# Attention followed by two feed-forward blocks: the halves of a head's values summed by a DMA in SBUF, and x loaded as one operand

## The chip, the cores and the metric

One core of one Trainium2 chip. The metric is device time in microseconds of one execution, lower is better. The engines are named as the profile does: PE is TensorE's matmul, PEld its weight load, DVE is VectorE, ACT is ScalarE, POOL is GpSimd, SP is SyncE, which here only issues DMAs; SPq is its queue.

## What is computed

Attention over 4 batches of 8 heads, 576 positions of 64 values, with scores further than tau below a row's maximum dropped; then a gated feed-forward block (512 to 1536 to 512) and a bilinear one, on 2304 tokens, all in float32.

```python
scores = (q @ k.T) / sqrt(64)                       # per batch and head
thresh = scores.max(-1, keepdims=True) - tau
scores = where(scores >= thresh, scores, -1e9)
attn = exp(scores - scores.max(-1, keepdims=True))
attn = attn / (attn.sum(-1, keepdims=True) + 1e-9)
x = (attn @ v).transpose(0, 2, 1, 3).reshape(2304, 512)
g = x @ w_gate; x = (g * sigmoid(g) * (x @ w_val)) @ moe_w_out
out = (((x @ w1) * (x @ w2)) @ w3) @ moe2_w_out
```

## The kernel before

Each float32 operand is split into a high and a low part in a format that TensorE multiplies at full rate, and a product is three matmul passes (high by high, high by low, low by high). The split costs ScalarE a copy (the high part) and VectorE or POOL a subtraction (the low part).

*Attention* runs in 16 passes, one for each batch and pair of heads (`p`, batch `p // 4`, pair `p % 4`), of 9 tiles of 128 queries each. For a tile: scores (L440), row maximum while they are copied out (VectorE, L479), exponential (ScalarE, L488), threshold for two tiles at a time (POOL, L471), mask and row sum (VectorE, L498; it stands two tiles behind the scores). The masked probabilities are turned by TensorE (L326) and split as they leave PSUM (L510 to L536), and multiplied with the values (L579, L584). The values stand as two parts side by side in the weights, so the result of a head has 128 rows: 64 from the high part of the values, 64 from the low part. ScalarE copies it into `xs` (L591, two buffers), and SP stores the two halves into `x_dram[0]` and `x_dram[1]` in DRAM (L595), two DMAs per head, four per pass. The reciprocal row sums of a batch go into `r_dram` (`it_norm`, L610 and L613).

Meanwhile the operands of the next pass are prepared: q and k are loaded (L281), turned, split, and stacked by twelve SBUF-to-SBUF DMAs (L349, L350: R<-khi, R<-klo, L<-qhi, L<-qlo) on SP. Rows of the profile with `L` and `R` are these tiles; `P` holds the scores, `AT` the turned probabilities.

*The first feed-forward block* reads x as blocks of 512, 512, 256, 512 and 512 tokens, each in four parts of 128 features: 20 preparations, `x_prep(j, kk)`. One takes two operand slots; SP loads both halves of x into the one (L785) and the reciprocal sums, spread over 64 rows, into the other (L790); POOL adds the halves (L821), VectorE multiplies by the reciprocals (L824), ScalarE writes the high part (L812), VectorE the low part (L813). The first four preparations are queued in the last pass of attention, the others in the entry into the block, between the steps `glu_step`: the projections (L830), the gate (L914, L915, and the split L107, L108), and the output products, accumulated in PSUM and added to SBUF by VectorE (L877) or, at first, copied by ScalarE (L879). Weights are loaded raw and split beside it (L140 to L200; `raw`, `tmp`).

*What sets the order.* The kernel issues the work of a pass through two queues of items with credits (`some`): `main` for the turning and the products, `prep` for the next pass's operands. A framework then simulates the program and fixes an order for each engine; on the chip each engine runs its own list in that order, and an instruction that waits holds up all that stand behind it. A DMA is issued by the engine whose list it stands in, when that engine comes to it. At the start `LZ` and `VLZ` are filled with zeros (L249, L253), and tau is loaded and its sign and positive part are taken (L656, L659).

Of the kernel before, what the change touches and what calls it, by code (L numbers as in the profile page):

```python
# [9 lines left out]
F32 = mybir.dt.float32  # L10
# [4 lines left out]
ALU = mybir.AluOpType  # L15
# [21 lines left out]
def kernel(  # L37
# [42 lines left out]

    x_dram = dram.tile([2, DM, B, S], F32, name="x_dram")
    r_dram = dram.tile([B, H, S], F32, name="r_dram")
# [151 lines left out]
    def attention(actx, early, tail):  # L234
# [13 lines left out]
        LZ = at.tile([P, 2, 3 * P], F32R, name="LZ")  # L248
        nc.gpsimd.memset(f32(LZ), 0.0)  # L249

        VLZ = [at.tile([P, HP, 2, 2, D], F32R, name=f"VLZ{n}") for n in range(2)]
        for t in VLZ:
            nc.gpsimd.memset(f32(t), 0.0)  # L253

# [314 lines left out]
        def it_pv(p, h, n):  # L569
# [22 lines left out]
            if n == 1:  # L592
                g = 2 * hp + h
                for e in range(2):
                    nc.sync.dma_start(  # L595
                        out=x_dram[e, g * D:(g + 1) * D, b, :], in_=xs[64 * e:64 * e + 64, :]
                    )

# [54 lines left out]
        load_left(0)  # L653
        nc.sync.dma_start(out=tau_sb, in_=tau.to_broadcast([P, 1]))

# [49 lines left out]
        for n, (p, i) in enumerate(tiles):  # L705
            b, hp = divmod(p, HP)
            if i == 0:
# [6 lines left out]
                if p + 1 < NP:  # L714
                    prep.extend(prep_items(p + 1))
                    credit[1] = 0.0
            if i == NTILE - 2:
# [62 lines left out]
    def x_load(j, kk):  # L780
        c0, n = blocks[j]
        x_raw[j, kk] = [take(F32) for _ in range(2)]
        tt, rg = x_raw[j, kk]
        for o, b, c, m in segs(c0, n):
            nc.sync.dma_start(  # L785
                out=tt[:, :, o:o + m],
                in_=x_dram[:, kk * P:(kk + 1) * P, b, c:c + m].rearrange("e p c -> p e c"),
            )
            for h in range(2):
                nc.sync.dma_start(  # L790
                    out=rg[64 * h:64 * h + 64, 0, o:o + m],
                    in_=r_dram[b, 2 * kk + h:2 * kk + h + 1, c:c + m].to_broadcast([64, m]),
                )
        return tt, rg

# [21 lines left out]
    def x_prep(j, kk):  # L817
        c0, n = blocks[j]
        tt, rg = x_load(j, kk)
        xr = tmp()  # L820
        nc.gpsimd.tensor_tensor(  # L821
            out=xr[:, 0:n], in0=tt[:, 0, 0:n], in1=tt[:, 1, 0:n], op=ALU.add
        )
        nc.vector.tensor_tensor(out=xr[:, 0:n], in0=xr[:, 0:n], in1=rg[:, 0, 0:n], op=ALU.mult)  # L824
        give(*x_raw.pop((j, kk)))
        x_split(j, kk, xr[:, 0:n])
# [299 lines left out]
```

## Time and profile before

| what | value |
|---|---|
| time, median of 3 runs | 1182.14 us (1175.77 to 1183.02) |
| the profiled execution's own time | 1180.05 us |
| its span in the trace | 1177.6 us |
| mean granted clock of TensorE | 0.993 |
| PE, PEld busy | 1112.7 us (94%), 952.4 us (81%) |
| DVE, ACT, POOL busy | 747.4 us (63%), 577.8 us (49%), 443.2 us (38%) |

The profiled execution is one run of the same program. Its span begins with its first instruction and ends with its last; the other 2.45 us of its time lie around the span. All rows below are of this execution. Attention ends at about 349 us; the entry into the first feed-forward block reaches to about 440 us.

### The profile page before, as it was taken

Reading aid. Unit: us, or ns where it says so; the run is one execution under the profiler, and the core shown is the slowest. Engines: PE = TensorE matmul, PEld = TensorE weight load, DVE = VectorE, ACT = ScalarE, POOL = GpSimd, SP = SyncE. Lnnn points to the kernel's source line nnn. Section 1 sums busy time; section 2 is a strip of 40 time slices with the busy share of each in tenths; the row PEclk is TensorE's granted clock in tenths of the full one; section 3 lists DMA queues with packets and bytes.
Section 4 is the critical chain, followed back from the end, with each engine's and each line's share of the span. In section 5 each row is a group of like instructions: output and inputs, shape, how many; then the busy total and the mean of one; then the engine's idle time right before and its main releaser. Section 6 shows DMA issues by size and latency. Waiting matters only on the chain.

```text
span 1177.6 us, 16738 instructions
## 1 busy us (share of the span) xinstructions
PE 1112.7 (94%) x6044; PEld 952.4 (81%) x6044; DVE 747.4 (63%) x1317; ACT 577.8 (49%) x1041; POOL 443.2 (38%) x434
## 2 busy tenths in 40 slices
PE   6898879989988899999999999999999999999998
PEld 5787779888876688888888888888787888888886
DVE  7999898999986786665463655477891122522222
ACT  5787777878876355434232432344662231321111
POOL 5456355645444555343241432234342221321110
PEclk9999999999999999999999999999999999999999
DMA  9865675755555832221120120133330010100023
GB/s 212 191 137 131 148 165 120 179 131 133 136 160 141 247 105 90 90 72 54 36 58 32 54 72 19 42 99 99 119 109 18 1 36 1 36 1 1 1 60 101
DMA packets 105330, 107.07 MB, mean 91 GB/s; under 512 B 48288, under 2 KB 79648, under 8 KB 105248
## 3 DMA queue, kind: packets, MB, share of 16 engines
q1 hardware_dynamic: 105248, 106.01, 34.4%
q8 instruction: 47, 0.77, 0.3%
q14 instruction: 35, 0.29, 0.1%
HBM read 68.16 MB, written 14.23 MB: 70 GB/s over the span
## 4 chain that ended last, share of the span: by engine, by line
PE 64%; DVE 17%; DMA 8%; issue 3%; POOL 2%; SPq 2%; ACT 2%; DVEq 0%; POOLq 0%; ACTq 0%
PE t_bank L830 36%; PE s_bank L830 19%; DVE P L498 4%; PE t_bank L579 4%; DVE P L479 3%; PE s_bank L440 2%; DMA raw<-in_moe_w_dram 2%; DMA L<-qlo 2%; PE t_bank L326 2%; DVE slot L813 1%; DMA slot<-r_dram 1%; DVE tmp L158 1%; PE t_bank L584 1%; DMA slot<-x_dram 1%; DVE tmp L824 1%
## 5 line engine op out<-in xcount | busy, mean ns | idle before, releaser
L830 PE MATMUL t_bank<-slot,slot 128*128 128x512 f32 (+1 forms) x2592 | 561.1, 372 | 5.7 <-DVE slot L813 2.0
L830 PEld LDWEIGHTS t_bank<-slot,slot 128*128 128x128 f32 x2592 | 458.3, 189 | 92.2 <-DVE slot L813 3.0
L830 PE MATMUL s_bank<-h,slot 128*128 128x512 f32 (+1 forms) x720 | 161.2, 371 | 7.2 <-DVE slot L877 3.6
L151 POOL TENSOR_TENSOR raw<-raw 128x512 int32<-128x512 int32 x76 | 85.1, 1120 | 191.2 <-ACT raw L150 181.6
L830 PEld LDWEIGHTS s_bank<-h,slot 128*128 128x128 f32 x720 | 126.8, 190 | 31.4 <-ACT tmp L914 3.7
L498 DVE SCALAR_TENSOR_TENSOR P<-P,stat,E 128x576 f32<-128x576 f32 x144 | 144.5, 1017 | 12.0 <-POOL stat L471 7.2
L1062 DVE TENSOR_TENSOR tmp<-tmp,t_bank 128x512 f32<-128x512 f32 (+1 forms) x40 | 25.4, 634 | 178.2 <-PE t_bank L830 178.2
L488 ACT ACTIVATE E<-P,stat 128x576 f32<-128x576 f32 x144 | 113.7, 792 | 28.9 <-DVE P L479 26.5
L108 POOL TENSOR_TENSOR h<-tmp,h 128x512 fp32r<-128x512 f32 (+1 forms) x60 | 74.9, 1248 | 127.0 <-ACT h L107 127.0
L1066 POOL TENSOR_TENSOR h<-tmp,h 128x512 fp32r<-128x512 f32 (+1 forms) x38 | 45.8, 1205 | 200.8 <-ACT h L1064 200.8
L479 DVE TENSOR_SCALAR_CACHE_REDUCE P<-s_bank,neg 128x576 f32<-128x576 f32 x144 | 114.9, 807 | 8.1 <-PE s_bank L440 7.4
L440 PE MATMUL s_bank<-R,L 128*128 128x288 f32 x512 | 99.3, 315 | 21.9 <-DVE P L479 10.1
L830 PE MATMUL s_bank<-slot,h 128*128 128x512 f32 x432 | 106.6, 391 | 0.9 <-DVE slot L1052 0.8
L915 DVE TENSOR_TENSOR tmp<-tmp,t_bank 128x512 f32<-128x512 f32 (+1 forms) x60 | 37.9, 632 | 107.1 <-PE t_bank L830 100.4
L440 PEld LDWEIGHTS s_bank<-R,L 128*128 128x128 f32 x512 | 74.3, 190 | 33.1 <-DVE P L479 18.2
L326 PE MATMUL t_bank<-ident,P 128*128 128x128 f32 x640 | 92.3, 278 | 9.2 <-DVE klo L343 2.9
L830 PEld LDWEIGHTS s_bank<-slot,h 128*128 128x128 f32 x432 | 79.9, 188 | 18.3 <-DVE slot L1052 2.1
L877 DVE TENSOR_TENSOR slot<-s_bank,slot 128x1024 f32<-128x1024 f32 (+1 forms) x72 | 82.5, 1147 | 18.5 <-PE s_bank L830 16.5
L158 DVE SCALAR_TENSOR_TENSOR tmp<-tmp,raw 128x512 f32<-128x512 f32 x76 | 68.9, 906 | 40.0 <-POOL raw L151 40.0
L326 PEld LDWEIGHTS t_bank<-ident,P 128*128 128x128 f32 x640 | 73.3, 141 | 18.7 <-DVE klo L343 4.4
L149 ACT ACTIVATE raw<-raw,ebias 128x512 int32<-128x512 int32 x76 | 58.0, 765 | 59.9 <-DVE tmp L146 47.4
L914 ACT ACTIVATE tmp<-t_bank 128x512 f32<-128x512 f32 (+1 forms) x60 | 33.3, 555 | 109.9 <-PE t_bank L830 104.2
(103 smaller groups left out, 1393.6 us busy)
## 6 DMA issues: line engine op xcount, KB each, us to landing
raw<-in_moe_w_dram SPq DMA_DIRECT2D x32, 512.0 KB, 3.8
raw<-in_moe_w_out_dram SPq DMA_DIRECT2D x20, 512.0 KB, 3.5
x_dram<-xs SPq DMA_DIRECT2D x64, 144.0 KB, 2.4
L<-qlo SPq DMA_DIRECT2D x60, 128.0 KB, 2.6
L<-qhi SPq DMA_DIRECT2D x60, 128.0 KB, 2.6
raw<-in_moe_w_gate_dram SPq DMA_DIRECT2D x12, 512.0 KB, 3.9
raw<-in_moe_w_val_dram SPq DMA_DIRECT2D x12, 512.0 KB, 3.8
ld<-in_k_dram SPq DMA_DIRECT2D x16, 256.0 KB, 3.6
```

Of the source, the lines that this page charges most:

```text
L108: nc.gpsimd.tensor_tensor(out=lo, in0=src, in1=f32(hi), op=ALU.subtract)
L149: nc.scalar.activation(out=a, in_=x, func=ACTF.Relu, scale=8.0, bias=ebias[:, 0:1])
L151: nc.gpsimd.tensor_tensor(out=a, in0=a, in1=x, op=ALU.subtract)
L158: nc.vector.scalar_tensor_tensor(out=f32(m), in0=f32(m), scalar=2.0 ** 20, in1=f32(a), op0=ALU.add, op1=ALU.mult)
L326: nc.tensor.matmul(bank[:, t * P:(t + 1) * P], lhsT=part, rhs=ident, is_transpose=True, start=(t == 0), stop=(t == len(parts) - 1),)
L440: nc.tensor.matmul(o, lhsT=lhs, rhs=R[:, c:c + HALF], start=(h == hs2[0] and e == 0), stop=(h == hs2[-1] and e == 1),)
L479: nc.vector.tensor_scalar(out=p_tile(p, i).rearrange("p (a c) -> p a c", a=2), in0=sb[:, :, 0:HALF], scalar1=neg, scalar2=None, op0=ALU.mu ...
L488: nc.scalar.activation(out=e, in_=p_tile(p, i), func=ACTF.Exp, scale=-1.0, bias=stats[p // HP][:, 0, c:c + 1],)
L498: nc.vector.scalar_tensor_tensor(out=t, in0=t, scalar=stats[b][:, 1, c:c + 1], in1=e, op0=ALU.is_le, op1=ALU.mult, accum_out=sums[b][:, c: ...
L579: nc.tensor.matmul(o, lhsT=vs[:, 4 * h + c, :, :].rearrange("p a d -> p (a d)"), rhs=AT[h][:, e, c, cs], start=(c == 0 and e == 0), stop=F ...
L830: nc.tensor.matmul(o, lhsT=lhs(a), rhs=rhs(c), start=(first and i == 0), stop=(last and i == 2))
L877: nc.vector.tensor_tensor(out=a, in0=s, in1=a, op=ALU.add)
```

## The change

- `x_dram` has one half. Once both parts of a head's `xs` are copied, POOL issues a DMA that adds rows 64 to 127 of `xs` onto rows 0 to 63 within SBUF, and SP stores rows 0 to 63. Per pass two DMAs on POOL and two on SP stand for four on SP.
- `x_load` takes one slot: x in its first half, the reciprocals in its second. The POOL add is gone; VectorE multiplies the two halves of the slot.
- The zero fills of `LZ` and `VLZ` go from POOL to VectorE.
- The load of tau goes from SP's queue to ScalarE's.
- The credit of the preparation queue starts at -1.5 instead of 0 in pass 0, so the operands of pass 1 are prepared later in it.

```diff
-    x_dram = dram.tile([2, DM, B, S], F32, name="x_dram")
+    x_dram = dram.tile([DM, B, S], F32, name="x_dram")
...
-        nc.gpsimd.memset(f32(LZ), 0.0)
+        nc.vector.memset(f32(LZ), 0.0)
...
-            nc.gpsimd.memset(f32(t), 0.0)
+            nc.vector.memset(f32(t), 0.0)
...
                 g = 2 * hp + h
-                for e in range(2):
-                    nc.sync.dma_start(
-                        out=x_dram[e, g * D:(g + 1) * D, b, :], in_=xs[64 * e:64 * e + 64, :]
-                    )
+                nc.gpsimd.dma_start(out=xs[0:64, :], in_=xs[64:P, :], accum_op=ALU.add)
+                nc.sync.dma_start(out=x_dram[g * D:(g + 1) * D, b, :], in_=xs[0:64, :])
...
-        nc.sync.dma_start(out=tau_sb, in_=tau.to_broadcast([P, 1]))
+        nc.scalar.dma_start(out=tau_sb, in_=tau.to_broadcast([P, 1]))
...
-                    credit[1] = 0.0
+                    credit[1] = 0.0 if p else -1.5
...
-        x_raw[j, kk] = [take(F32) for _ in range(2)]
-        tt, rg = x_raw[j, kk]
+        t = x_raw[j, kk] = take(F32)
         for o, b, c, m in segs(c0, n):
             nc.sync.dma_start(
-                out=tt[:, :, o:o + m],
-                in_=x_dram[:, kk * P:(kk + 1) * P, b, c:c + m].rearrange("e p c -> p e c"),
+                out=t[:, 0, o:o + m], in_=x_dram[kk * P:(kk + 1) * P, b, c:c + m]
             )
             for h in range(2):
                 nc.sync.dma_start(
-                    out=rg[64 * h:64 * h + 64, 0, o:o + m],
+                    out=t[64 * h:64 * h + 64, 1, o:o + m],
...
-        tt, rg = x_load(j, kk)
+        t = x_load(j, kk)
         xr = tmp()
-        nc.gpsimd.tensor_tensor(
-            out=xr[:, 0:n], in0=tt[:, 0, 0:n], in1=tt[:, 1, 0:n], op=ALU.add
-        )
-        nc.vector.tensor_tensor(out=xr[:, 0:n], in0=xr[:, 0:n], in1=rg[:, 0, 0:n], op=ALU.mult)
-        give(*x_raw.pop((j, kk)))
+        nc.vector.tensor_tensor(
+            out=xr[:, 0:n], in0=t[:, 0, 0:n], in1=t[:, 1, 0:n], op=ALU.mult
+        )
+        give(x_raw.pop((j, kk)))
```

How the change moves the lists of the engines, at three places. A row is the line, the operation, output <- inputs and the shape; in the changed kernel the lines behind the edits are 2 to 5 lower (L824 is L817, L813 is L809, L915 is L910, L877 is L872; L594 is the accumulating DMA).

POOL where pass 6 ends and pass 7 begins; `sp` are the values' high and low parts of the next pass. Before:

```order
L104 TENSOR_TENSOR AT<-tmp,AT 128x512
L471 TENSOR_SCALAR stat<-stat,tau_sb 128x2
L101 TENSOR_SCALAR sp_2673<-ld_2093 128x8x64
L104 TENSOR_TENSOR sp_2673<-ld_2093,sp_2673 128x8x64
L471 TENSOR_SCALAR stat<-stat,tau_sb 128x2
```

The changed kernel, at the same place:

```order
L471 TENSOR_SCALAR stat<-stat,tau_sb 128x2
L594 DMA xs<-xs 64x576
L101 TENSOR_SCALAR sp_2673<-ld_2093 128x8x64
L104 TENSOR_TENSOR sp_2673<-ld_2093,sp_2673 128x8x64
L594 DMA xs<-xs 64x576
L471 TENSOR_SCALAR stat<-stat,tau_sb 128x2 x2
```

The two accumulating DMAs stand among the thresholds; each waits for ScalarE's copy of its `xs`, and two thresholds follow the second.

SP where pass 7 ends, the end of the second batch. Before:

```order
L595 DMA x_dram<-xs 64x576 x4
L610 DMA r_dram<-rt 8x4x128
L613 DMA r_dram<-rt 8x1x64
L274 DMA ld_2971<-in_v_dram 128x2x256
L281 DMA ld_3033<-in_k_dram 128x8x64
L281 DMA ld_3035<-in_q_dram 128x8x64
L349 DMA R<-khi 64x512
L350 DMA R<-khi 64x512
```

The changed kernel, at the same place:

```order
L595 DMA x_dram<-xs 64x576
L608 DMA r_dram<-rt 8x4x128
L611 DMA r_dram<-rt 8x1x64
L274 DMA ld_2971<-in_v_dram 128x2x256
L281 DMA ld_3033<-in_k_dram 128x8x64
L595 DMA x_dram<-xs 64x576
L349 DMA R<-khi 64x512
L350 DMA R<-khi 64x512
```

The four stores became two, and the second, which waits for its accumulate, stands right ahead of the twelve stacking DMAs.

VectorE in the entry into the first feed-forward block, at the preparations of the third and fourth block of tokens. Before:

```order
L824 TENSOR_TENSOR tmp<-tmp,slot_5098 128x256
L813 TENSOR_TENSOR slot_5080<-tmp,slot_5080 128x256
L824 TENSOR_TENSOR tmp<-tmp,slot_5111 128x256
L915 TENSOR_TENSOR tmp<-tmp,t_bank 128x512
L813 TENSOR_TENSOR slot_5081<-tmp,slot_5081 128x256 x2
L824 TENSOR_TENSOR tmp<-tmp,slot_5174 128x512
L915 TENSOR_TENSOR tmp<-tmp,t_bank 128x512
L824 TENSOR_TENSOR tmp<-tmp,slot_5191 128x512
L813 TENSOR_TENSOR slot_5184<-tmp,slot_5184 128x512
```

The changed kernel, at the same place:

```order
L817 TENSOR_TENSOR tmp<-slot_5077 128x256
L817 TENSOR_TENSOR tmp<-slot_5088 128x256
L809 TENSOR_TENSOR slot_5062<-tmp,slot_5062 128x256 x2
L809 TENSOR_TENSOR slot_5063<-tmp,slot_5063 128x256 x2
L910 TENSOR_TENSOR tmp<-tmp,t_bank 128x512
L817 TENSOR_TENSOR tmp<-slot_5149 128x512
L809 TENSOR_TENSOR slot_5158<-tmp,slot_5158 128x512
L817 TENSOR_TENSOR tmp<-slot_5164 128x512
L910 TENSOR_TENSOR tmp<-tmp,t_bank 128x512
```

The multiplies read a landed slot instead of POOL's sum, and stand a little further ahead of the subtractions.

## Rows read from the trace of the kernel before

**Rows 1.** The page, busy time, share of the span and instructions of each engine.

```profile
PE 1112.7 (94%) x6044; PEld 952.4 (81%) x6044; DVE 747.4 (63%) x1317; ACT 577.8 (49%) x1041; POOL 443.2 (38%) x434
```

**Rows 2.** Windows: length, busy PE PEld DVE ACT POOL (instructions), clock, DMA share, GB/s.

```profile
15.00:330.00 315.00, 280.10 (x2010) 253.50 (x2011) 292.43 (x661) 250.76 (x499) 161.55 (x193) 0.99 0.65 151
...
350.00:380.00 30.00, 25.44 (x134) 20.62 (x135) 19.78 (x29) 19.83 (x35) 10.68 (x8) 0.98 0.54 145
380.00:396.00 16.00, 14.93 (x62) 11.93 (x61) 10.48 (x14) 6.58 (x11) 9.34 (x9) 0.92 0.78 221
396.00:413.00 17.00, 12.71 (x68) 10.99 (x69) 14.36 (x20) 5.98 (x13) 10.98 (x9) 0.91 0.90 256
...
440.00:800.00 360.00, 359.89 (x1764) 304.71 (x1764) 206.76 (x278) 138.99 (x223) 127.47 (x107) 1.00 0.19 59
```

**Rows 3.** Lines by form, 350 to 440 us: busy us, mean ns, idle before.

```profile
L821 POOL TENSOR_TENSOR tmp<-slot 128x512 f32<-128x512 f32 x12 | 17.5, 1464 | 15.0 <-DMA slot<-r_dram 10.8 <-DMA slot<-x_dram 3.0 <-DVE slot L813 1.2
...
L824 DVE TENSOR_TENSOR tmp<-tmp,slot 128x512 f32<-128x512 f32 x13 | 15.1, 1172 | 4.7 <-POOL tmp L821 3.3 <-DMA slot<-r_dram 1.3
L813 DVE TENSOR_TENSOR slot<-tmp,slot 128x512 fp32r<-128x512 f32 x13 | 14.5, 1120 | 0.9 <-ACT slot L812 0.7
```

**Rows 4.** Timeline of DVE: start, length, instruction, idle before and its releaser.

```profile
402.54 0.68 DVE L824 TENSOR_TENSOR tmp<-tmp,slot 128x512 f32<-128x512 f32 x1
403.14 3.46 DVE L813 TENSOR_TENSOR slot<-tmp,slot 128x512 fp32r<-128x512 f32 x2
...
414.38 1.78 DVE L824 TENSOR_TENSOR tmp<-tmp,slot 128x512 f32<-128x512 f32 x1
```

**Rows 5.** Lines by form, DVE, 440 to 640 us.

```profile
L200 DVE TENSOR_TENSOR slot<-tmp,slot 128x512 fp32r<-128x512 f32 x11 | 9.8, 888 | 6.0 <-ACT slot L197 6.0
```

**Rows 6.** Timeline of PE in the entry.

```profile
378.35 0.73 PE L830 MATMUL s_bank<-h,slot 128*128 128x512 f32 x2 [1.91 <-ACT h L107]
...
408.82 2.07 PE L830 MATMUL s_bank<-h,slot 128*128 128x512 f32 x6 [3.57 <-DVE slot L877]
```

**Rows 7.** Timeline of POOL at the end of attention.

```profile
345.30 1.50 POOL L821 TENSOR_TENSOR tmp<-slot 128x512 f32<-128x512 f32 x1 [3.87 <-DMA slot<-x_dram]
346.79 0.29 POOL L471 TENSOR_SCALAR stat<-stat,tau_sb 128x2 f32<-128x2 f32 x1
```

**Rows 8.** Timeline of POOL where a pass ends.

```profile
203.47 1.28 POOL L104 TENSOR_TENSOR sp<-ld,sp 128x512 fp32r<-128x512 f32 x1
```

**Rows 9.** Timeline of SP's queue at the same boundary.

```profile
209.68 0.65 SPq L349 DMA_DIRECT2D R<-khi  x1
```

**Rows 10.** Waits, 15 to 330 us: in total us, times, longest us.

```profile
PE s_bank L440 <- DMA L<-qlo: 7.6, 9, 2.4
...
DVE P L498 <- POOL stat L471: 5.8, 11, 1.4
...
SPq L595 <- ACT xs L591: 68.8, 24, 6.5
```

**Rows 11.** DMA issues, 15 to 330 us: KB each, median us to landing.

```profile
x_dram<-xs SPq DMA_DIRECT2D x56, 144.0 KB, 2.4
...
R<-klo SPq DMA_DIRECT2D x30, 128.0 KB, 3.8
```

**Rows 12.** Timelines of PE and DVE behind the stack of that boundary.

```profile
216.53 0.37 PE L440 MATMUL s_bank<-R,L 128*128 128x288 f32 x1 [1.30 <-DMA L<-qhi]
...
218.65 0.95 PE L440 MATMUL s_bank<-R,L 128*128 128x288 f32 x6
...
220.30 0.81 DVE L479 TENSOR_SCALAR_CACHE_REDUCE P<-s_bank,neg 128x576 f32<-128x576 f32 x1
```

**Rows 13.** Timelines of POOL and DVE at the start.

```profile
0.86 0.74 POOL L249 MEMSET LZ<- 128x768 f32 x1
1.54 1.84 POOL L253 MEMSET VLZ<- 128x1024 f32 x2
...
3.62 0.90 DVE L392 TENSOR_SCALAR slot<-ld 128x256 fp32r<-128x256 f32 x4 [2.73 <-DMA ld<-in_k_dram]
```

More of the change, by code (lines that the diff above doesn't have):

```diff
@@ L790, in x_load @@
                 nc.sync.dma_start(
-                    out=rg[64 * h:64 * h + 64, 0, o:o + m],
+                    out=t[64 * h:64 * h + 64, 1, o:o + m],
                     in_=r_dram[b, 2 * kk + h:2 * kk + h + 1, c:c + m].to_broadcast([64, m]),
                 )
-        return tt, rg
+        return t
     def x_views(j):
```

## The prediction

> **What bounds the kernel now.** The order of reading was: the page's busy line, the busy times by stretch, and then, inside the one stretch where no engine is full, the groups of instructions, the waits and the timelines.
>
> The busy line puts TensorE at 1112.7 of 1177.6 us [rows 1]. That is an average over stages with different limits. By stretch [rows 2], three things differ. From 15 to 330 us (attention) VectorE is busy 292.43 of 315 us and sets the pace; TensorE has 280.10. From 440 to 800 us TensorE is busy 359.89 of 360 us: nothing that happens on another engine can help there. Between them, from 350 to 413 us, lies the entry into the GLU block, and there nobody is full: TensorE is busy 25.44 of 30, 14.93 of 16 and 12.71 of 17 us, so it idles 4.56 + 1.07 + 4.29 = 9.9 us. In the same three rows the granted clock is 0.98, 0.92 and 0.91. The clock has two levels, 2.4 GHz and half of it, so a mean of 0.92 over 16 us is 2 x 0.08 x 16 = 2.6 us at half clock; the three rows make 1.2 + 2.6 + 3.1 = 6.8 us, which cost half, 3.4 us. **The most that a smoother entry can give is 9.9 + 3.4 = 13.3 us.** The change works in two places: this entry (the preparation of x) and attention (the stores of x).
>
> **Part 1, the preparation of x.** The change takes away twenty POOL adds (L821), one of the two operand slots of each preparation and half of the bytes read from x_dram; the DVE multiply then reads the landed tile directly. What the add costs now: from 350 to 440 us the twelve 512-wide ones take 17.5 us, 1464 ns each, and the DVE multiply and subtraction of the same preparation (L824, L813) take 1172 and 1120 ns in the mean [rows 3]. Undisturbed, L824 takes 0.68 us, at 402.54; at 414.38 the same shape takes 1.78 [rows 4]. So a VectorE instruction with two SBUF inputs grows while POOL is at work. If all thirteen went at 0.68, that is 13 x 0.49 = 6.4 us for L824 and 13 x 0.44 = 5.7 us for L813: 12 us of VectorE in 90. The gain is less, because POOL still has the L108 and L151 of this stretch. How much less, L200 shows: the same shape as L813, from 440 to 640 us, when L821 is no longer there, takes 888 ns [rows 5]. At 0.89 the saving is 13 x (0.28 + 0.23) = 6.6 us. With it the hop over POOL goes: VectorE stood 3.3 us in this stretch for L821 [rows 3].
>
> The Trainium skill, page "SBUF — State Buffer", section "Who interferes with whom", says that a VectorE instruction with two SBUF inputs contends with a GpSimd instruction that reads SBUF, whichever is second standing still. The pair 0.68 and 1.78 us agrees; by the rule alone L158, L813 and L817 go on colliding with L108 and L151, which is the 0.89 end of the sum, not the 0.68 end.
>
> What TensorE waits for: at 408.82 it stood 3.57 us for the accumulation L877, which on VectorE was queued behind L824 and the two L813 that took 3.46 us together [rows 4, 6]. In the changed order the pairs stand in the same places with the multiplies ahead, and the adds are gone from POOL. I therefore give it about three quarters of the 13.3 us: **-10 us** (bounds: -4, where only this stall shrinks, and -13). A stall goes, and the next to be late is ScalarE or the weights' conversion; TensorE's 1.9 us for ScalarE's h at 378.35 [rows 6] I leave in place.
>
> **Part 2, the end of attention.** The last pass has the first preparations in it. There the threshold L471 stood behind an L821 of 1.50 us that itself had waited 3.87 us for x, and the mask behind it came late [rows 7]. Without L821 this goes: **-2 us** (0 to -3).
>
> **Part 3, the accumulating DMA on POOL.** There are 32, two per pass, each 144 KB. No row of before shows a DMA issued from POOL. Its cost on POOL is bounded by the cheapest POOL instruction near it, 0.29 us [rows 7], and the dearest, 1.28 [rows 8]; I take what an issue on SP takes, about 0.65 [rows 9]. That makes 21 us on an engine which is busy 161.55 of 315 [rows 2], so the load itself is covered. It counts only where L471 is queued behind it. In the new order the second accumulate of a boundary stands right ahead of two L471, and it waits for ScalarE's copy of xs, as the store on SP does now, 68.8 us in 24 waits [rows 10]. POOL will come there later than SP did, so most of that wait is over by then. VectorE now stands 5.8 us, 11 times, for L471 [rows 10]. Were the second accumulate of each of fifteen boundaries to push the masks by its 0.65 us, it would be 10 us; were all covered, nothing. Since POOL mostly waits for the maximum at L471 and not the other way, I take **+2 us** (0 to +10).
>
> **Part 4, the store on SP.** Of four stores per pass two go, which frees 2 x 0.65 us of SP. But each of the two left waits until its accumulate has landed, and behind it in SP's queue stand the twelve DMAs that stack the next pass's operands. How long from issue to landing: bounds are 2.4 us, the same bytes out to x_dram, and 3.8, the slowest SBUF-to-SBUF group, R<-klo [rows 11]; an accumulate also reads its destination, so I take 3.4. At the boundary shown, POOL is free for the second accumulate at 203.47 + 1.28 = 204.75 [rows 8]; with 0.65 + 3.4 it lands at 208.80, and the store issues until 209.45. The stack begins at 209.68 [rows 9]: hidden, by 0.2 us. Past that the whole stack moves, and the scores move with it: TensorE already stood 1.30 us at 216.53 for L<-qhi; the tile's last matmuls come at 218.65, about 219.0, and VectorE takes the first maximum at 220.30 [rows 12], a slack of 1.3 us. So at this boundary landing in up to 3.4 + 0.2 + 1.3 = 4.9 us costs nothing. At nine other places TensorE waits for L<-qlo, 7.6 us in all [rows 10], and less slack is left; there I put 0.35 us each: **+3 us** (0 to the rival below). ScalarE's copies into xs have a second buffer, which is a pass's half away, and cost nothing.
>
> The Trainium skill, page "DMA: Bandwidth & Descriptors", section "Anatomy of one DMA — SWDGE (gpsimd) path", fits 2.0 us plus bytes over 436 GB/s; an estimate by that page is 2.34 us for 147,456 bytes, at which Part 4 would be 0. No row of before shows it.
>
> **Part 5, the start and the credit.** The zero fills take 0.74 + 1.84 us on POOL; on VectorE, at the same length, they fit in the 2.73 us that it waits for k [rows 13]. tau, on ScalarE's queue, no longer follows the loads on SP. **0** (-0.5 to +0.5). The credit of pass 1's preparation leaves the order of the matmuls nearly as it was: 0, with 0.5 either way.
>
> **The sum.** -10 - 2 + 2 + 3 + 0 = -7 us against the profiled execution's own 1180.05, which lies 2 us under the median of 1182.14: **1173 us**.
>
> **The rivals.**
> *The accumulate lands late (slower).* If it needs over 4.9 us from issue to landing, the head of SP's queue blocks the stack past the slack worked out above. At 7.6 us, twice the 3.8 of the slowest group, each boundary loses 2.7 us; over the nine with a wait today 24 us, over all fifteen 40. With the gain of 12 kept, 1180 + 2 + 24 - 12 = 1194, up to 1210. For it speaks that POOL must issue while VectorE is busy 93% of attention [rows 2], against it that POOL's own instructions in the rows are hardly stretched. The turning point is a landing of about 6.0 us (1.1 us lost at nine places, 10 in all, which with POOL's 2 is the 12 gained).
>
> The Trainium skill, page "SBUF — State Buffer", section "🔬 SBUF: two separate sides", warns of this: a DMA from the GpSimd queue has its descriptors written by GpSimd, which is locked out while VectorE runs in a two-port mode. No row of before has such a DMA; by the rule this rival would be the likely one wherever VectorE runs such an operation.
>
> *Attention gives back what the entry gains.* POOL at +10 and SP at +3 against -12: 1181.
>
> *The entry does not gain.* If ScalarE or the conversion of weights is what ends last once VectorE is freed, only the -4 of the stall stays and -2 + 5 around it: 1179. For it speaks TensorE's wait for ScalarE's h at 378.35 [rows 6], which names no preparation; against it, the 12 us of stretched VectorE time.
>
> **How the numbers follow.** Forecast 0.55, by itself 1163 to 1178; accumulate late 0.20 (1188 to 1210); given back 0.13 (1178 to 1184); no gain 0.12 (1177 to 1183). A measurement of this kernel tells about 1%, 12 us, from no change. Of the forecast's 0.55 some 0.30 lies below 1168, where the entry gives its full 13 and attention takes nothing, and the rest with the two middle cases is within 1%, 0.50; of the late accumulate 0.17 lies over 1192 and 0.03 under it. 8 in 10 is 1162 to 1195.
>
> **What would show it.** In the entry: L817 near 0.7 to 0.9 us, TensorE's idle time from 350 to 413 down from 9.9 to about 2, the clock at 1.0. In attention: the accumulate's landing under 5 us, the first R<-khi of a boundary no later than before, VectorE's wait for L471 under 8 us. The forecast is wrong if the attention stage ends later than 355 us or if TensorE's idle time in the entry stays.

## The result and the profile after

The changed kernel takes 1193.27 us (median of 4 runs, 1191.62 to 1198.55), the kernel before 1180.27 beside it: a ratio of 1.0105 [1.0075, 1.0135]. The time lies in the range given, near its upper end, and on the other side than forecast: 12 us slower instead of 7 faster. The profiled execution took 1191.62 us, its span is 1189.7, the mean granted clock 0.985.

The page of after, the busy line (us, share of the span, instructions) and the accumulating DMA among its issues (KB each, us to landing), which answer to [rows 1, 11]:

```profile
PE 1120.2 (94%) x6044; PEld 959.6 (81%) x6044; DVE 741.5 (62%) x1320; ACT 578.1 (49%) x1041; POOL 437.9 (37%) x443
...
xs<-xs POOLq DMA_DIRECT2D x32, 144.0 KB, 3.2
```

VectorE and POOL are busy for less time than before and TensorE for 7.5 us more, at a lower clock. The busy line does not tell where 12 us went; the stretches do.

After, busy times by stretch (columns as in [rows 2]). The three rows of the entry begin 11.6 us later than those of [rows 2], because the last mask of attention ends at 360.27 us instead of 348.67:

```profile
15.00:330.00 315.00, 277.83 (x1948) 249.66 (x1946) 284.37 (x638) 244.16 (x485) 174.19 (x215) 0.97 0.66 146
...
361.60:391.60 30.00, 25.33 (x132) 21.03 (x130) 13.90 (x27) 19.73 (x36) 5.51 (x6) 0.94 0.33 83
391.60:407.60 16.00, 15.74 (x64) 12.69 (x65) 10.07 (x17) 7.06 (x14) 6.48 (x5) 0.89 0.65 188
407.60:424.60 17.00, 13.72 (x75) 11.82 (x74) 11.72 (x18) 7.20 (x14) 4.41 (x4) 0.90 0.67 193
```

In attention VectorE, which sets the pace there, did 8 us less work in the same 315 us: 284.37 instead of 292.43. It waited. In the entry TensorE idles 4.7 + 0.3 + 3.3 = 8.2 us instead of 9.9, and by the clock of these rows it spends 10.5 us at half speed instead of 6.8: little was gained there in this kernel. Followed by the start of each pass's first row maximum (passes are counted from 0), the loss grows in steps: +0.8 us at pass 5, +4.8 at pass 6, +8.2 at pass 8, +11.8 at pass 11, +11.6 at the last mask. At the 400th matmul of the feed-forward block it is +9.3.

After, the waits from 15 to 330 us (total us, times, longest):

```profile
POOL xs L594 <- ACT xs L591: 18.4, 9, 6.0
DVE P L479 <- PE s_bank L440: 17.7, 13, 5.1
...
DVE P L498 <- POOL stat L471: 7.0, 8, 2.2
```

The new instruction, L594, is POOL's DMA, and POOL stands for ScalarE's copy ahead of it. VectorE's wait for scores, L479 for L440, is 17.7 us in 13 waits; it was 7.4 in 8. Its wait for the threshold has hardly grown, 7.0 after 5.8 [rows 10]. That points to the scores, which need the stack of operands behind SP's store. How much is the store's, this row does not tell: with the same lists and no accumulating DMA at all, VectorE waits 12.7 and 12.4 us for scores (the first and the seventh run below), so only some 5 us of the growth need the DMA.

### The profile page after: what moved, and what is told of

Read it like the earlier page. It is cut to its first block, busy times and chain, and to the rows that moved or that the text cites. A ratio compares the mean times of both kernels' runs of the same rounds, so it can differ in the third digit from the quotient of the medians.

```text
span 1189.7 us, 16745 instructions
## 1 busy us (share of the span) xinstructions
PE 1120.2 (94%) x6044; PEld 959.6 (81%) x6044; DVE 741.5 (62%) x1320; ACT 578.1 (49%) x1041; POOL 437.9 (37%) x443
## 4 chain that ended last, share of the span: by engine, by line
PE 71%; DVE 13%; DMA 5%; ACT 3%; issue 3%; SPq 2%; POOL 2%; DVEq 0%; POOLq 0%; ACTq 0%
PE t_bank L825 39%; PE s_bank L825 20%; PE t_bank L579 5%; DVE P L498 4%; PE s_bank L440 3%; DVE P L479 3%; PE t_bank L326 2%; DMA raw<-in_moe_w_dram 2%; DMA slot<-r_dram 1%; PE t_bank L584 1%; SPq L786 1%; DMA L<-qlo 1%; DVE slot L809 1%; ACT E L488 1%; DVE tmp L158 1%
## 5 line engine op out<-in xcount | busy, mean ns | idle before, releaser
L498 DVE SCALAR_TENSOR_TENSOR P<-P,stat,E 128x576 f32<-128x576 f32 x144 | 143.8, 1013 | 9.0 <-POOL stat L471 7.9
L479 DVE TENSOR_SCALAR_CACHE_REDUCE P<-s_bank,neg 128x576 f32<-128x576 f32 x144 | 115.1, 808 | 18.2 <-PE s_bank L440 17.7
L440 PE MATMUL s_bank<-R,L 128*128 128x288 f32 x512 | 100.7, 318 | 20.6 <-DVE P L479 10.7
L910 DVE TENSOR_TENSOR tmp<-tmp,t_bank 128x512 f32<-128x512 f32 (+1 forms) x60 | 37.9, 632 | 117.7 <-PE t_bank L825 115.2
L440 PEld LDWEIGHTS s_bank<-R,L 128*128 128x128 f32 x512 | 76.5, 194 | 33.8 <-DVE P L479 23.2
L872 DVE TENSOR_TENSOR slot<-s_bank,slot 128x1024 f32<-128x1024 f32 (+1 forms) x72 | 82.4, 1147 | 18.6 <-PE s_bank L825 16.5
L326 PEld LDWEIGHTS t_bank<-ident,P 128*128 128x128 f32 x640 | 75.7, 145 | 19.1 <-DVE klo L343 3.0
```

Source lines behind the costliest of these rows:

```text
L326: nc.tensor.matmul(bank[:, t * P:(t + 1) * P], lhsT=part, rhs=ident, is_transpose=True, start=(t == 0), stop=(t == len(parts) - 1),)
L440: nc.tensor.matmul(o, lhsT=lhs, rhs=R[:, c:c + HALF], start=(h == hs2[0] and e == 0), stop=(h == hs2[-1] and e == 1),)
L479: nc.vector.tensor_scalar(out=p_tile(p, i).rearrange("p (a c) -> p a c", a=2), in0=sb[:, :, 0:HALF], scalar1=neg, scalar2=None, op0=ALU.mu ...
L498: nc.vector.scalar_tensor_tensor(out=t, in0=t, scalar=stats[b][:, 1, c:c + 1], in1=e, op0=ALU.is_le, op1=ALU.mult, accum_out=sums[b][:, c: ...
L872: nc.vector.tensor_tensor(out=a, in0=s, in1=a, op=ALU.add)
```

## The experiments

Two theories stood against each other. **By the DMA:** the accumulate costs POOL time, and the store that waits for it costs time at the head of SP's queue; the preparation without the add gains what was forecast. **By the order (O):** the framework, simulating another program, fixed lists for the engines that happen to be worse, and the DMA itself is hidden. To part them, most kernels here have the list of every engine fixed, to that of after or to that of before; then only the instruction in question differs. Ratios are to the kernel before, run beside; 0.1% is 1.18 us.

**The accumulate taken out, lists of after.**

```diff
-                nc.gpsimd.dma_start(out=xs[0:64, :], in_=xs[64:P, :], accum_op=ALU.add)
```

> The changed kernel without its 32 accumulating DMAs; every engine's list is fixed to the one of the changed kernel, with those DMAs left out, so the stores wait for ScalarE's copies alone (the low half is never added, the output lacks it). Theory W, the accumulate costs attention directly, by its issue on POOL and by SP's wait for its landing ahead of the stack: the 9 us that attention lost between its first and its last maximum come back, 1184 us. Theory O, the lists that the scheduler wrote for the changed program are the worse ones, and the waits themselves are covered: 1191 us or more, within 2 us of the changed kernel.

1174.54 us, 0.9929 [0.9907, 0.9952]. With the very lists of after, but without the DMA, the kernel is 8.4 us faster than before, more than either theory had allowed (1184, and 1191 or more): the order is not what costs. Its last mask ends at 348.56 us, as before's does (348.67), and the 400th matmul of the feed-forward block comes at 451.43 instead of 458.58: the gain lies in the entry.

**Thirteen stores put off.** On SP's list the second store of passes 0 to 12 stands behind the next twelve stacking DMAs (L349, L350); nothing else moves.

> The changed kernel whole, its lists fixed, with one thing moved: in SP's list the second store of each of the first 13 passes stands behind the next twelve stacking DMAs instead of ahead of them, so that its wait for the accumulate holds up no stack. Theory W in its form on SP (head of the queue): the stack starts about 0.9 us earlier after khi at each boundary, and 4 to 8 us come back, 1185 to 1189 us. Theory O: nothing comes back, 1192 us. Theory W in its form on POOL (the 0.86 us issue and the wait for xs ahead of L471): nothing comes back here either, but does where the accumulates are left out.

1186.15 us, 1.0027 [1.0013, 1.0042]. That is 0.78% under the changed kernel, 9 us by the ratios, with some 4 either way; the two recorded executions differ by 5.0 us of span. So the place of one store on SP costs time. But it is not most of the loss in attention: at most boundaries the stack is now issued almost as soon as its operands are ready, and the last mask still ends at 358.37 us, 1.9 earlier than in the changed kernel and 9.7 later than before. SP still waits 79.9 us for accumulates there, with other DMAs behind it.

**The lists of before, accumulate and store put in.** The start's edits and the credit are left out, each accumulate is put into POOL's list behind the end of its `xs` in the trace of before, each store some 3.3 us behind that; the entry is free.

> The accumulate, the one store per head and the one-operand preparation, without the edits of the start and of the credit; up to the first load of x every engine's list is that of the kernel before, with each accumulate put into POOL's list behind ScalarE's copy and each store into SP's list some 3.3 us later, by the times of the trace before; behind it the scheduler is free. Theory W: attention ends 5 to 10 us later than before, total 1182 to 1188 us. Theory O: attention ends within 2 us of before and the entry keeps a gain of 2 to 10, total 1170 to 1178 us.

1199.76 us, 1.0145 [1.0114, 1.0176], later than both theories had it and slower than the changed kernel. The order that suited before does not suit the DMA. Together with the first run this fells the theory of the order: lists of after without the DMA are faster than before, lists of before with it are slower than after.

**The cost of the add alone, lists of before.**

```diff
-            out=xr[:, 0:n], in0=tt[:, 0, 0:n], in1=tt[:, 1, 0:n], op=ALU.add
+            out=xr[:, 0:8], in0=tt[:, 0, 0:8], in1=tt[:, 1, 0:8], op=ALU.add
...
-        nc.vector.tensor_tensor(out=xr[:, 0:n], in0=xr[:, 0:n], in1=rg[:, 0, 0:n], op=ALU.mult)
+        nc.vector.tensor_tensor(out=xr[:, 0:n], in0=rg[:, 0, 0:n], in1=rg[:, 0, 0:n], op=ALU.mult)
```

> The kernel before with every list fixed as it was; the POOL add L821 works on 8 columns instead of 512 or 256, and VectorE multiplies the reciprocals by themselves, so two operands in SBUF are read as before (the output is not x). It takes away the add's time on POOL and its contention, and nothing else. If contention with the add stretches VectorE and so sets the entry, as I forecast: L824 and L813 near 0.7 to 0.9 us, 6 to 10 us gained, 1170 to 1174 us. If something else ends last in the entry: 0 to 3 us gained, 1177 to 1180 us.

1173.58 us, 0.9936 [0.9916, 0.9956]: -7.6 us with POOL's add made short; the multiply reads the reciprocals twice, so that it keeps two inputs in SBUF, and the output is not x. Its groups of instructions by line and shape, 350 to 440 us, answer to [rows 3]:

```profile
L821 POOL TENSOR_TENSOR tmp<-slot 128x8 f32<-128x8 f32 x16 | 5.3, 344 | 22.0 <-DMA slot<-x_dram 18.0 <-DMA slot<-r_dram 4.0
...
L824 DVE TENSOR_TENSOR tmp<-slot 128x512 f32<-128x512 f32 x13 | 11.4, 891 | 8.6 <-DMA slot<-r_dram 6.0 <-POOL tmp L821 1.5 <-issue 1.0
L813 DVE TENSOR_TENSOR slot<-tmp,slot 128x512 fp32r<-128x512 f32 x14 | 10.4, 744 | 1.2 <-ACT slot L812 0.9
```

VectorE's multiply falls from 1172 to 891 ns and its subtraction from 1120 to 744, though neither has less to do: the difference is time that POOL's add took from VectorE.

**The changed kernel once more**, beside the next three.

> The changed kernel once more, unchanged, as the anchor for the three beside it: 1.0% over before, about 1193 us. Nothing is decided by it but how far the others of this set are from it.

1193.43 us, 1.0104 [1.0066, 1.0143].

**The same DMA, but nobody waits for it** (lists of after). It adds the lower half onto the upper, which nothing reads, so the store follows ScalarE's copy as it did before.

```diff
-                nc.gpsimd.dma_start(out=xs[0:64, :], in_=xs[64:P, :], accum_op=ALU.add)
+                nc.gpsimd.dma_start(out=xs[64:P, :], in_=xs[0:64, :], accum_op=ALU.add)
```

> The changed kernel with its lists fixed; each accumulating DMA adds rows 0 to 63 onto rows 64 to 127, which nobody reads, so it is issued and moves its bytes as before but no store waits for it (the output lacks the low half). If POOL's issue and its wait for xs ahead of the thresholds is what costs: most of the 19 us between the changed kernel and the one without the DMAs stays, 1186 us or more. If the store's wait at the head of SP's queue costs: 1174 to 1178 us. The stores moved late gave back 7 us, so I expect some 12 us over the kernel without the DMAs: 1186 us.

1182.45 us, 1.0003 [0.9984, 1.0022]. Against the changed kernel that is 1.0% less: about 12 us by the ratios, with some 4 either way, are the store's wait. The spans of the two recorded executions differ by 9.2 us.

**POOL waits, but issues no DMA** (lists of after).

```diff
-                nc.gpsimd.dma_start(out=xs[0:64, :], in_=xs[64:P, :], accum_op=ALU.add)
+                nc.gpsimd.tensor_scalar(
+                    out=xs[64:P, 0:8], in0=xs[64:P, 0:8], scalar1=1.0, scalar2=None, op0=ALU.mult
+                )
```

> The changed kernel with its lists fixed; in the place of each accumulating DMA stands a POOL multiplication by one over 64 x 8 numbers of the half of xs that nobody reads: POOL waits for ScalarE's copy of xs at the same place, but issues no DMA (the output lacks the low half). If the wait for xs ahead of the thresholds costs: as the run in which nobody waits for the DMA, some 1186 us. If the issue itself costs (0.86 us of POOL, 32 times, and what VectorE or the DMA engines lose to it): 1175 to 1177 us, as without the DMAs.

1174.06 us, 0.9931 [0.9907, 0.9956], as without any accumulate. So POOL's standing for ScalarE costs nothing, and the step from here to the run above, 0.72% or 8.5 us (8.0 by the spans), is what a DMA on POOL costs in place of a multiplication of 0.27 us.

The three runs at one boundary, between passes 5 and 6. The changed kernel (timeline of SP, ScalarE, TensorE and VectorE; start, length, instruction, idle before and its releaser):

```profile
119.66 0.50 SPq L595 DMA_DIRECT2D x_dram<-xs  x1
...
121.93 0.61 ACT L341 ACTIVATE khi<-t_bank 128x512 fp32r<-128x512 f32 x1
...
123.76 0.67 SPq L349 DMA_DIRECT2D R<-khi  x1
...
132.84 0.50 PE L440 MATMUL s_bank<-R,L 128*128 128x288 f32 x2 [3.33 <-DMA L<-qlo]
...
137.36 0.95 PE L440 MATMUL s_bank<-R,L 128*128 128x288 f32 x6
...
137.96 0.82 DVE L479 TENSOR_SCALAR_CACHE_REDUCE P<-s_bank,neg 128x576 f32<-128x576 f32 x1 [5.92 <-PE s_bank L440]
```

The same place where POOL waits but issues no DMA:

```profile
118.05 0.50 SPq L597 DMA_DIRECT2D x_dram<-xs  x1
...
122.18 0.62 ACT L341 ACTIVATE khi<-t_bank 128x512 fp32r<-128x512 f32 x1
...
122.83 0.54 SPq L349 DMA_DIRECT2D R<-khi  x1
...
130.77 0.51 PE L440 MATMUL s_bank<-R,L 128*128 128x288 f32 x2
...
134.48 0.82 DVE L479 TENSOR_SCALAR_CACHE_REDUCE P<-s_bank,neg 128x576 f32<-128x576 f32 x1 [0.89 <-PE s_bank L440]
```

And where the DMA is issued but nobody waits for it:

```profile
122.05 0.58 SPq L349 DMA_DIRECT2D R<-khi  x1
...
130.89 0.60 PE L440 MATMUL s_bank<-R,L 128*128 128x288 f32 x2 [1.89 <-issue]
...
136.01 0.82 DVE L479 TENSOR_SCALAR_CACHE_REDUCE P<-s_bank,neg 128x576 f32<-128x576 f32 x1 [4.49 <-PE s_bank L440]
```

In the second, the stack begins when its operand is ready: khi ends at 122.80, R<-khi is issued at 122.83. In the first, khi ends at 122.54 and SP comes only at 123.76, since the store held it to 119.66 and five loads stand between. These 1.2 us have become 2.1 at TensorE's first scores (132.84 against 130.77) and 3.5 at VectorE's first maximum: the other six score matmuls stand on TensorE's list behind twenty products with the values, and in the first these run at a granted clock of 0.57, right after TensorE had stood 3.33 us. But the third shows that the store is not the whole of it: there the stack is on time too (khi ends at 122.03), and still TensorE stands 1.89 us, its next 4 us run at 0.57, and the maximum comes 1.5 us later than in the second.

Worked out from the timelines in the same way, the first R<-khi is issued later than its khi by 7.1 us summed over the fifteen boundaries in before, 9.5 where POOL waits but issues nothing, 14.2 where nobody waits for the DMA, 19.9 and 21.5 in the two runs of the changed kernel, and 6.4 where thirteen stores are put off. The last of these kernels has the least lateness of all and ends attention 9.7 us after before: a late stack is a part of the loss, not its measure.

SP's longest waits from 17 to 345 us, in the changed kernel's second run, where nobody waits for the DMA, and where there is none:

```profile
SPq L595 <- DMA xs<-xs: 105.4, 25, 9.9
```

```profile
SPq L595 <- ACT xs L591: 42.2, 12, 6.1
```

```profile
SPq L597 <- ACT xs L591: 42.0, 12, 8.5
```

The length of such a wait says little by itself: 68.8 us for `xs` stood in before [rows 10], beside a stack that was 7.1 us late in all. What counts is how much of it lies past the moment at which the operands of the DMAs behind it are ready.

The wait goes on into the entry. SP in the changed kernel's second run:

```profile
384.97 0.70 SPq L611 DMA_DIRECT2D r_dram<-rt  x1
388.00 0.47 SPq L595 DMA_DIRECT2D x_dram<-xs  x1
388.56 0.53 SPq L782 DMA_DIRECT2D slot<-x_dram  x1
```

and where POOL issues none:

```profile
370.92 0.47 SPq L597 DMA_DIRECT2D x_dram<-xs  x1
371.50 0.54 SPq L784 DMA_DIRECT2D slot<-x_dram  x1
```

SP stands 2.3 us, from 385.67 to 388.00, for the last accumulate, and the load of x for the next preparation (L782) stands behind it. From the last mask to this load it is 28.0 us above (from 360.60) and 22.5 below (from 349.04); where nobody waits for the DMA it is 22.6.

Where the time is lost, by the recorded executions (us; the 400th matmul is the feed-forward block's). The last mask of each is a row of VectorE's timeline, here of the runs in which POOL issues no DMA, nobody waits for it, thirteen stores are put off, and of the changed kernel:

```profile
348.22 0.82 DVE L498 SCALAR_TENSOR_TENSOR P<-P,stat,E 128x576 f32<-128x576 f32 x1 [0.34 <-ACT E L488]
```

```profile
355.49 0.82 DVE L498 SCALAR_TENSOR_TENSOR P<-P,stat,E 128x576 f32<-128x576 f32 x1 [0.32 <-ACT E L488]
```

```profile
357.55 0.82 DVE L498 SCALAR_TENSOR_TENSOR P<-P,stat,E 128x576 f32<-128x576 f32 x1 [0.31 <-ACT E L488]
```

```profile
359.45 0.82 DVE L498 SCALAR_TENSOR_TENSOR P<-P,stat,E 128x576 f32<-128x576 f32 x1
```

| kernel | last mask ends | from there to the 400th matmul | span |
|---|---|---|---|
| before | 348.67 | 109.9 | 1177.6 |
| POOL waits, no DMA | 349.04 | 102.7 | 1172.9 |
| DMA, nobody waits | 356.31 | 102.4 | 1180.9 |
| thirteen stores put off | 358.37 | 106.3 | 1184.7 |
| changed kernel, first and second run | 360.27, 360.60 | 107.6, 107.4 | 1189.7, 1190.1 |

So in attention the DMA on POOL costs 7.3 us and the store's wait 4.0 to 4.3, of which about 2 come back with the thirteen stores put off. The entry gains 7.2 us without the wait, and the wait takes about 5 of them back.

**The add at the load.** The stores of before, and the second half of x added as it is loaded, in the entry only.

```diff
+            src = x_dram[:, kk * P:(kk + 1) * P, b, c:c + m]
+            nc.sync.dma_start(out=t[:, 0, o:o + m], in_=src[0])
+            nc.gpsimd.dma_start(out=t[:, 0, o:o + m], in_=src[1], accum_op=ALU.add)
```

> The kernel before with its four stores per pass, its start and its credit; x is loaded into one slot, the low half by an accumulating DMA of POOL at the load, and the POOL add is gone. The scheduler is free. If the cost of the change is that of accumulating within attention, this keeps attention as before and the entry's gain of up to 9 us, less what the later landing of x costs: 1173 to 1178 us. If any accumulating DMA near busy VectorE is slow, the entry waits for x and the time is 1182 us or more.

1192.57 us, 1.0081 [1.0054, 1.0109]. Attention is then nearly as before (last mask +1.5 us), but the wait has moved to POOL's own list. Its row among the waits from 345 to 420 us:

```profile
POOL slot L786 <- DMA slot<-x_dram: 32.7, 14, 10.9
```

Behind L786 stand POOL's parts of the gate and of the weights, and the block's hundredth matmul comes 11.1 us later than in before.

**A tiny DMA, nobody waits** (lists of after): 64 rows of 8 values, 2 KB.

```diff
+                nc.gpsimd.dma_start(out=xs[64:P, 0:8], in_=xs[0:64, 0:8], accum_op=ALU.add)
```

> The changed kernel with its lists fixed; each accumulating DMA adds 64 x 8 numbers onto the half of xs that nobody reads, instead of 64 x 576 (the output lacks the low half): the issue on POOL stays, the bytes are gone, nobody waits. If the 8.4 us that the DMA costs without a waiting store are its issue on POOL (0.86 us, 32 times): 1180 to 1183 us. If they are the bytes, which share the 16 DMA engines with the stacking DMAs: 1174 to 1177 us.

1183.89 us, 1.0016 [0.9997, 1.0035]: as much as with 144 KB (1.0003) within the intervals. The bytes cost nothing that can be measured; the last mask ends at 354.72 us, against 356.31 with them. A POOL instruction of the same 0.85 us without a DMA was not run, so whether the time on POOL costs or the issuing is not separated. By line, the DMA issued from POOL, here and in the changed kernel (ns shortest/median/longest, first and last start):

```profile
L594 POOL DMA_DIRECT2D xs<-xs x32: 807/851/1094, 44.0 to 375.6; - x32
...
DMA to landing us min/median/max: 1.9/2.7/4.6
```

```profile
L594 POOL DMA_DIRECT2D xs<-xs x32: 810/859/1026, 44.7 to 384.1; - x32
...
DMA to landing us min/median/max: 2.8/3.2/6.1
```

**The start alone** (lists of before; zero fills on VectorE, tau on ScalarE's queue).

> The kernel before with every list fixed as it was, but for the edits of the start: the zero fills stand on VectorE behind its first two fills, tau is loaded at the head of ScalarE's queue. My forecast for them was 0 within 0.5 us: 1183 beside 1183. In the changed kernel the first maximum came 2.8 us later and the third pass no later than before; if what is lost at the start stays lost, this is 2 to 3 us slower, 1185.

1182.77 us, 1.0015 [1.0001, 1.0030]: +1.8 us. VectorE's first work on k (L392) starts at 5.27 us, waiting for the load of k, instead of 3.62 [rows 13]. Where 1.8 us would stay lost is not seen: in the recorded execution the first maximum comes 1.3 us later than in before, the second pass is on time again, and the last mask ends 0.9 us earlier. The credit alone, the remaining part of the change, was not run.

**The add on VectorE** instead of POOL, order free.

```diff
-        nc.gpsimd.tensor_tensor(
+        nc.vector.tensor_tensor(
             out=xr[:, 0:n], in0=tt[:, 0, 0:n], in1=tt[:, 1, 0:n], op=ALU.add
```

> The kernel before with the add of the two halves of x on VectorE instead of POOL, nothing else; the scheduler is free. VectorE has 0.68 us more per preparation if nothing contends, and loses the stretching by the add (some 0.5 us on the multiply, 0.4 on the subtraction). If contention is what the entry pays for, it gains a part of the 9 us of the run with the small add: 1175 to 1180 beside 1183. If VectorE's busy time bounds the entry: no gain, 1183 or more.

1179.91 us, 0.9991 [0.9976, 1.0005]: no change that can be measured. A likely reading is that VectorE now spends on the adds what POOL no longer takes from it; no row was taken to show it.

**One accumulate and one store per pass, the store written behind the stack.** One `xs` for both heads, one buffer, order free.

```diff
+                nc.gpsimd.dma_start(out=xs[0:64], in_=xs[64:P], accum_op=ALU.add)
+                late.append((xs, hp, b))
```

> The change with the start as before, and both heads of a pass in one xs tile: one accumulating DMA of 288 KB per pass instead of two of 144 KB, and one store, written behind the next pass's stacking DMAs. The scheduler is free. It halves the issues (8.4 us, to some 4) and takes the store from the head of the stack (11 us, to 0 to 4 with the last passes' part): 1176 to 1181 beside 1183, faster than before. If what costs is not the number of issues and the place of the store: 1190 as in the changed kernel.

1207.25 us, 1.0229 [1.0206, 1.0252]. It does not test the theory cleanly: the framework put the store ahead of the stack all the same. SP's wait for the one accumulate (17 to 400 us):

```profile
SPq L573 <- DMA xs<-xs: 43.6, 12, 15.0
```

Half as many waits, the longest 15.0 us, ahead of the stack as before, and VectorE waits 32.5 us for scores: the loss is larger, against a forecast of 1176 to 1181. Which part of it is the single buffer was not separated. No kernel that does the whole computation beats the kernel before.

## Why the prediction was wrong

**The sum, in one line.** The change without its DMA is worth -8.2 us, the DMA on POOL costs 8.5, the store's wait 12: +12.3. Forecast were -12, +2 and +3. The three terms are differences of neighbouring ratios, so they add up to the measured change by themselves; each is known to some 3 to 5 us. If the start's +1.8 carries over, it is in the -8.2.

**Part 1 and 2, the preparation and the end of attention: right, somewhat too large.** Forecast -12; measured -8.2, or -10 without the start's cost, and -7.6 for the shorter add alone. Part 2, the -2 at the end of attention, was not measured by itself. By line, 361 to 452 us, the multiply and the subtraction of the changed kernel are where they were expected (0.7 to 0.9 us):

```profile
L817 DVE TENSOR_TENSOR tmp<-slot 128x512 f32<-128x512 f32 x12 | 9.2, 780 | 8.5 <-DMA slot<-r_dram 8.2 <-issue 0.4
L809 DVE TENSOR_TENSOR slot<-tmp,slot 128x512 fp32r<-128x512 f32 x12 | 8.3, 710 | 1.1 <-ACT slot L808 1.0
```

TensorE's idle time from 350 to 413 us was to fall from 9.9 to about 2. It falls to 3.7 + 0 + 2.9 = 6.6 us where POOL waits but issues no DMA, and the time at half clock from 6.8 to 2 x 0.10 x 17 = 3.4 us (that kernel's busy times by stretch):

```profile
350.00:380.00 30.00, 26.32 (x143) 21.52 (x142) 16.74 (x28) 20.90 (x37) 7.21 (x8) 1.00 0.34 91
380.00:396.00 16.00, 16.00 (x83) 13.77 (x82) 11.34 (x18) 7.92 (x14) 5.32 (x4) 1.00 0.66 192
396.00:413.00 17.00, 14.11 (x66) 11.75 (x65) 14.89 (x22) 6.58 (x13) 4.15 (x4) 0.90 0.65 179
```

Part of what is left shows in the changed kernel's row of L817 above: VectorE now waits 8.2 us for the load of the reciprocals. Before, it was mostly POOL's add that waited for it, 10.8 us [rows 3].

**Part 3, the DMA on POOL: the term was mis-sized.** +2 forecast, 8.5 measured, inside its bounds of 0 to 10; 7.3 of it is in attention, where it is the larger of the two losses. The length of an issue was nearly right (0.86 us against SP's 0.65), and so was the place. The threshold was taken for the only path to VectorE; VectorE's wait for it stays near 7 us in all three runs. What else it goes over is in part open. From 17 to 362 us the 144 masks take 140.3 us where POOL issues no DMA, 144.9 with the tiny one and 146.5 with the full one: 5 to 6 us, which would be most of the loss. But this sum is no measure by itself: it is 144.5 us in before and 139.1 with the edits of the start alone, with no DMA on POOL in either, and attention ends only 0.9 us apart. The largest single growth, in the changed kernel's second run (timeline of VectorE and POOL):

```profile
230.23 1.03 POOL L594 DMA_DIRECT2D xs<-xs  x1
...
230.81 1.77 POOL L104 TENSOR_TENSOR sp<-ld,sp 128x512 fp32r<-128x512 f32 x1
230.92 4.08 DVE L498 SCALAR_TENSOR_TENSOR P<-P,stat,E 128x576 f32<-128x576 f32 x1
...
232.10 1.69 POOL L200 TENSOR_TENSOR slot<-tmp,slot 128x512 fp32r<-128x512 f32 x1
...
233.35 1.03 POOL L101 TENSOR_SCALAR AT<-tmp 128x512 fp32r<-128x512 f32 x1
```

The mask takes 4.08 us, five times its undisturbed 0.81, beside three POOL instructions in a row that the DMA had put off to here; where POOL issues none, the same mask takes 1.16 us. Where nobody waits for the DMA, it takes 4.08 us as well. That the DMA works mainly by moving POOL's other instructions against the masks is read from such places; no run isolates it. In the changed kernel itself, whose masks start later, they take 143.8 us, less than where nobody waits, so the two costs may overlap.

**Part 4, the store on SP: the step that failed most.** +3 forecast, 12 measured by the ratios, 9.2 by the recorded spans. The landing was right: 3.2 us in the median against 3.4. Two things failed. The larger is a term put at nothing without a reason: the last stores stand on SP ahead of the loads of x, and in the entry the wait costs about 5 us, which Part 4 did not look at. The smaller is the slack in attention. It was read at one boundary by the times of before and used for the other fourteen, less 0.35 us at nine; the sum, 3 us, came near the measured 4.0 to 4.3, but not for its reason. At the very boundary that was read, the accumulate was to start at 204.75, 2.2 us behind the end of its `xs` (202.50), and to be hidden. In the changed kernel POOL comes to it 3.2 us behind (`xs` ends at 209.10), since one more subtraction for the values stands ahead of it; over all 32 it is 0.3 to 3.2 us, and this comes on top of the landing. POOL, then SP there, to be held against [rows 8, 9]:

```profile
211.24 1.13 POOL L104 TENSOR_TENSOR VLZ<-vl,VLZ 64x256 fp32r<-64x256 f32 x1
212.32 0.85 POOL L594 DMA_DIRECT2D xs<-xs  x1
```

```profile
213.84 0.68 SPq L281 DMA_DIRECT2D ld<-in_k_dram  x1
215.62 0.49 SPq L595 DMA_DIRECT2D x_dram<-xs  x1
216.20 0.55 SPq L349 DMA_DIRECT2D R<-khi  x1
```

SP stands 1.1 us (214.52 to 215.62) with the stack right behind it, and the stack starts 1.8 us after its khi (214.44).

**Part 5, start and credit: near, the start above its bounds.** Forecast 0 with half a microsecond either way; the start measured +1.8 [0.1, 3.5], and the credit was not measured.

**The rivals.** The late accumulate has the result in its range (1188 to 1210), but not by its condition: it was to decide from a landing of 6.0 us on, and the median is 3.2. That 1193 lies in its range, and inside the whole range given, is luck: 8.5 of the 20 us are POOL's DMA, and about 5 more are lost in the entry. "Attention gives back what the entry gains" had POOL's price (10 against 8.5), but took SP's 3 from Part 4. Of the forecast's own signs, L817 (0.78 us), the landing and the wait for L471 (7.0 us) came as forecast; the first R<-khi came later, TensorE's idle time stayed at 8.2 us, and attention ended at 360.27 us, past the 355 that were to mark the forecast as wrong.

## What to carry to other kernels

Before a store is made to wait for a DMA, list what stands behind it on the issuing engine, and ask at every place where it occurs, in the new order, how long ago the operands of those entries are ready; the slack of one place says nothing of the others, nor of the next stage, whose first loads may stand behind the last stores. A wait on a queue that was free while its releaser came early turns into loss once it lasts past that moment, however little the new transfer takes. And price a new instruction on an engine that shares time with the pacing engine by a run without its payload (the same wait, the same lists, another instruction): here three such runs divided the 20 us between the changed kernel and the one without the DMA into 8.5 and 12, where the waits of the profile alone gave neither price.

## What the runs showed of the hardware

- A DMA issued from POOL has a span of 0.86 us on POOL in the median, 0.85 with 2 KB instead of 144, and the next POOL instruction can start before it ends (at 230.81 against 231.26 in the rows above); it lands 3.2 us after issue, 2.7 with 2 KB. An issue on SP takes 0.47 to 0.70 in the rows shown.
- A wait of the issuing engine for one DMA holds every later DMA of its list: 105.4 us of such waits on SP, and 12 us of time here. The Trainium skill, page "DMA: Bandwidth & Descriptors", section "Anatomy of one DMA — SWDGE (gpsimd) path", says that DMA engines do not wait on semaphores, the issuing sequencer does, before dispatch; the runs agree.
- The accumulates landed in 2.8 to 6.1 us while VectorE was busy 284 of 315 us: a landing of 7.6 us, as the first rival had it, was not seen. The Trainium skill, page "SBUF — State Buffer", section "🔬 SBUF: two separate sides", says that GpSimd is locked out of writing a DMA's descriptors while VectorE runs in a two-port mode; no run here shows such a hold-up, and none tells which of VectorE's instructions here run in that mode.
- A VectorE instruction with two SBUF inputs grew to 4.08 us beside POOL instructions in a row, so it can lose more time than one of them takes (the longest took 1.77).
- TensorE, released after 3.33 us of standing, ran the next 4 us at a granted clock of 0.57, so for the most part at the lower of its two levels (1.2 GHz), at one boundary of the changed kernel; where nobody waits for the DMA it did so after 1.89 us, and where POOL issues none it did not stand and ran at 1.00. Stretches at half clock come and go between kernels with equal lists, too: from 15 to 330 us the granted clock is 0.99 in before and 0.97 with the short add and the same lists, and attention ends 2.1 us apart. So no total is put down to them here.
